# Two early attention batches by head halves and tile pairs, and another order of the first loads

## The chip, the cores and the metric

The kernel runs on one core of one Trainium2 chip. The metric is the device time in microseconds (us) from the start to the end of one execution; lower is better. The core has the engines PE (matrix products), DVE, ACT and POOL (element-wise work), and SP, which here only issues DMA. POOL issues DMA too, in a queue of its own, for transfers that change the type on the way. Every engine works through its own queue in order and waits at semaphores for the others.

## The reference

Linear attention with cosine weights, then a gated feed-forward layer. B, H, S, D are 8, 8, 576, 64; the layer goes from 512 to 2048 and back.

```python
theta = np.pi / 2.0 * np.arange(S) / S
def phi(x, c, s):
    r = np.maximum(x, 0.0)
    return np.concatenate([r * c, r * s], axis=-1)
q_p, k_p = phi(q, cos_w, sin_w), phi(k, cos_w, sin_w)
kv = np.einsum('bhsf,bhsd->bhfd', k_p, v)
z = np.sum(k_p, axis=2)
num = np.einsum('bhsf,bhfd->bhsd', q_p, kv)
den = np.einsum('bhsf,bhf->bhs', q_p, z)[..., None] + 1e-06
x = (num / den).transpose(0, 2, 1, 3).reshape(B * S, H * D)
h = x @ w_in
out = (h * np.cos(h)) @ w_out
```

## The kernel before

Each batch of 576 rows is cut into four tiles of 128 tokens and a rest of 64; the rests of all batches form a ninth batch for the layer alone. For one batch the steps are: SP loads q, k, v in float32 (`load`, L318 and L321, two DMAs each; v of batches 0 and 1 in two halves of four heads). DVE or ACT makes a feature from a tile (`prep`, L346 on ACT, L347 on DVE: relu, times the cosine or sine column, 512 wide for eight heads). v is cast to 16 bits (`cast_v`, L360 to L362). PE transposes q's features (`q_pe`, L402) and ACT or DVE copies them out of PSUM into `qT` (L406, L408). PE sums k's features times v over the tiles (`kv`, L373), and the sum goes to `kvz` (L385, L387, L390). PE multiplies `qT` by `kvz` (`num`, L435); DVE adds 1e-6 to the denominator, takes its reciprocal and multiplies (L451, L453, L455: the norm, into `x16`). PE transposes the result (`x_pe`, L475) and ACT copies it to `xT` (L479). Layer 1 of batches 0 and 1 (`layer1`, L529) makes blocks of eight matmuls of 256 columns; ACT takes the cosine (L502), DVE multiplies (L504) into `gT`. Layer 2 of batch 0 (`layer2_plain`, L786) makes blocks of eight matmuls of 512 columns, four with the first half of `w_out` and four with the second; ACT stores the first half's sum (L794), DVE adds the second (L797). Later batches use Strassen-like products: sums of weights (`w_out_sums`, L809; `w_in_sums`, L603) and L667, L679, L861, L872, L883.

PSUM has eight banks: three `M1`, two `M2`, one `TR`, two `ATT`. `num` of batches 0 and 1 uses `ATT` and, by turns, a pair of the others.

The order is written out. Each step is added to a plan with the engines that may do it; the tables `STARTS` and `ENGS` give each step its place and its engine, and steps are issued in the order of `STARTS`. What a step waits for follows from the data it reads and writes.

Batch 0 loads q, k, v in this order. While they come, PE runs matmuls on constants (`warm`, L945: 28, then 17, then 9 more between the steps of `num`). POOL copies an element of k into `w_in_sb` (L950): this makes the four loads of `w_in` (L956) wait for k. A copy of a loaded element of `w_in` in the same way releases half of `w_out` (L960, L970). An element of `w_in`'s third quarter releases batch 1's loads (`hold_raw`, L975), and an element of batch 1's q the second half of `w_out` (`part_of_w_out`, L982).

## Time and profile before

| | |
|---|---|
| three timed runs, us | 281.47, 281.58, 283.69; median 281.58 |
| profiled execution: its span, us | 279.7 |
| instructions | 6825 |
| PE, DVE, ACT, POOL busy, us | 272.6, 236.9, 210.2, 82.9 |
| warm-up matmuls of L945 | 9.04 us for the first 28, 3.67 us for the next 17 |
| HBM read and written, MB | 36.75 and 11.80 |
| DMA queue of POOL, of SP | 17.04 MB and 39.99 MB |

The profile is of one execution; of its own time the page gives the span alone, which lies 1.9 us under the median of the timed runs. PE's busy time holds the warm-up matmuls, which compute nothing. Line numbers L are those of the kernel before, up to the result. "Idle before, releaser" names what an engine waited for. The time of a DMA is counted from its issue to its landing, so a wait in a queue is in it.

### The profile page before, as it was taken

How to read it: one execution, taken by the hardware profiler on the slowest of the kernel's cores; microseconds unless marked ns; L12 is line 12 of the kernel's file. 1: busy time of each engine (PE TensorE's matmuls, PEld its weight loads, DVE VectorE, ACT ScalarE, POOL GpSimd, SP SyncE). 2: the span in 40 equal slices, each digit the busy share in tenths (PEclk: the TensorE clock that was granted, in tenths of full speed). 3: DMA queues.
4: the chain of work that ended last, by engine and by line, in shares of the span. 5: the costliest groups of instructions: out<-in, count | busy, mean ns of one | idle time of the engine just before them, and what ended most of it. 6: DMA issues, size and time to landing. Idle time of an engine off the chain costs nothing.

```text
span 279.7 us, 6825 instructions
## 1 busy us (share of the span) xinstructions
PE 272.6 (97%) x2698; PEld 215.5 (77%) x2698; DVE 236.9 (85%) x442; ACT 210.2 (75%) x363; POOL 82.9 (30%) x102
## 2 busy tenths in 40 slices
PE   8999999999999999999999999999999999999993
PEld 2567857787966677769777878789988888888882
DVE  1767698989999999999999998989989879873952
ACT  2756699879998897788989988995758686776330
POOL 1430020030501201520340045132534372399210
PEclk9999999999999999999999999999999999999999
DMA  6999989999999999989999998549756495698125
GB/s 207 312 202 206 340 239 241 361 301 174 335 261 271 258 249 246 234 268 259 255 258 246 242 229 284 98 115 141 163 75 139 110 156 105 152 143 123 75 77 150
DMA packets 80223, 58.03 MB, mean 207 GB/s; under 512 B 43200, under 2 KB 77248, under 8 KB 80192
## 3 DMA queue, kind: packets, MB, share of 16 engines
q1 hardware_dynamic: 68960, 39.99, 59.4%
q0 software_dynamic: 10496, 17.04, 30.1%
q10 hardware_dynamic: 736, 0.57, 0.7%
q8 instruction: 21, 0.34, 0.5%
q14 instruction: 10, 0.08, 0.1%
HBM read 36.75 MB, written 11.80 MB: 174 GB/s over the span
## 4 chain that ended last, share of the span: by engine, by line
PE 92%; ACT 3%; DVE 2%; issue 1%; POOL 0%; ACTq 0%; POOLq 0%
PE M L861 34%; PE M L667 14%; PE M L561 11%; PE M L529 9%; PE TR L667 6%; PE ATT L945 5%; PE ATT L435 3%; PE M L786 3%; PE ATT L373 3%; PE TR L561 2%; ACT KQ L346 2%; DVE x L455 1%; PE M L402 1%; PE M L373 0%; PE TR L475 0%
## 5 line engine op out<-in xcount | busy, mean ns | idle before, releaser
L861 PEld LDWEIGHTS <-gT 128*128 128x128 f16 x560 | 53.9, 98 | 8.3
L861 PE MATMUL M<-w_out_sb,gT 128*128 128x256 f16 x448 | 57.1, 273 | 0.0
L504 DVE TENSOR_TENSOR gT<-M,ch 128x512 f16<-128x512 f32 x73 | 48.5, 685 | 5.9 <-ACT ch L502 5.7
L502 ACT ACTIVATE ch<-M 128x512 f32<-128x512 f32 x75 | 43.4, 596 | 12.0 <-PE M L529 5.4
L346 ACT ACTIVATE KQ<-km,CS 128x512 f16<-128x512 f32 x57 | 38.5, 717 | 1.4 <-DMA km<-in_k_dram 1.3
L872 ACT ACTIVATE ost<-M 128x512 f32<-128x512 f32 x41 | 24.3, 596 | 17.9 <-PE M L861 13.0
L346 ACT ACTIVATE KQ<-qm,CS 128x512 f16<-128x512 f32 x46 | 31.5, 720 | 4.1 <-DMA qm<-in_q_dram 4.1
L561 PE MATMUL M<-xT,w_in_sb 128*128 128x512 f16 x136 | 33.8, 379 | 0.0
L861 PE MATMUL M<-T,S 128*128 128x256 f16 x256 | 32.4, 273 | 0.0
L667 PEld LDWEIGHTS <-w_in_sb 128*128 128x128 f16 x288 | 27.3, 98 | 4.8 <-issue 0.3
L362 POOL CAST V<-vm 128x1024 f16<-128x1024 f32 (+1 forms) x18 | 15.9, 907 | 50.8 <-DVE den L451 20.7
L529 PE MATMUL M<-xT,w_in_sb 128*128 128x256 f16 x256 | 30.3, 273 | 0.3 <-DVE gT L504 0.3
L861 PEld LDWEIGHTS <-S 128*128 128x128 f16 x256 | 24.8, 98 | 4.1 <-DVE S L837 0.2
L529 PEld LDWEIGHTS <-w_in_sb 128*128 128x128 f16 x256 | 24.4, 98 | 3.9 <-issue 0.5
L679 DVE TENSOR_TENSOR Z<-M,Z 128x512 f32<-128x512 f32 x31 | 21.1, 687 | 4.3 <-PE M L667 3.1
L561 PEld LDWEIGHTS <-w_in_sb 128*128 128x128 f16 x160 | 14.9, 98 | 12.2
L504 POOL TENSOR_TENSOR gT<-Z,ch 128x512 f16<-128x512 f32 x5 | 6.3, 1268 | 56.6 <-ACT ch L502 20.0
L455 DVE TENSOR_TENSOR x<-ATT,rec 128x512 f16<-128x512 f32 x32 | 22.1, 691 | 1.1
L435 PEld LDWEIGHTS <-qT 128*128 128x128 f16 (+1 forms) x320 | 14.8, 101 | 5.6 <-issue 3.5
L690 ACT ACTIVATE ch<-Z 128x1024 f32<-128x1024 f32 x12 | 12.7, 1057 | 6.9 <-DVE Z L679 4.8
L675 ACT ACTIVATE Z<-M 128x512 f32<-128x512 f32 x26 | 15.1, 596 | 3.4 <-PE M L667 2.4
L435 PE MATMUL ATT<-kvz,qT 128*128 128x65 f16 (+1 forms) x288 | 16.0, 195 | 0.8 <-DVE x L455 0.5
(150 smaller groups left out, 519.3 us busy)
## 6 DMA issues: line engine op xcount, KB each, us to landing
out_dram<-ost POOLq DMA_DIRECT2D x38, 256.0 KB, 4.3
qm<-in_q_dram SPq DMA_DIRECT2D x8, 640.0 KB, 6.7
km<-in_k_dram SPq DMA_DIRECT2D x8, 640.0 KB, 7.1
qm<-in_q_dram SPq DMA_DIRECT2D x8, 512.0 KB, 6.0
km<-in_k_dram SPq DMA_DIRECT2D x8, 512.0 KB, 6.0
vm<-in_v_dram SPq DMA_DIRECT2D x6, 640.0 KB, 5.7
vm<-in_v_dram SPq DMA_DIRECT2D x6, 512.0 KB, 4.6
w_in_sb<-in_moe_w_in_dram POOLq DMA_DIRECT2D x4, 512.0 KB, 8.8
```

The source lines that it names most:

```text
L346: fn = {"ACT": lambda: nc.scalar.activation(out=out_, in_=in_, func=AF.Relu, scale=sc), "DVE": lambda: nc.vector.tensor_scalar(out=out_, i ...
L362: "POOL": lambda: nc.gpsimd.tensor_copy(out=out_, in_=in_)}
L435: nc.tensor.matmul(bank[hb][ps, hh * D1:(hh + 1) * D1], lhsT=x[:, h, :], rhs=z[:, h, :], start=True, stop=True)
L455: nc.vector.tensor_tensor(out=split(x16[n][:, hs, :], k), in0=A[:, :, :, 0:D], in1=split(rec[n][:, hs], k).unsqueeze(3).broadcast_to((P, k ...
L502: act(0.5, due, lambda: nc.scalar.activation(out=ch[c], in_=bank, func=AF.Sin, bias=math.pi / 2.0, scale=1.0), [key], [("ch", c)])
L504: mul(due, 0.61, lambda q: q.tensor_tensor(out=dst, in0=bank if len(dst.shape) == 2 else bank.rearrange("p (j s) -> p j s", j=dst.shape[1] ...
L529: nc.tensor.matmul(M1[m][:, jj * 2 * P:(jj + 1) * 2 * P], lhsT=w_in_sb[:, cc, j * P:(j + 1) * P], rhs=X[:, cc, ts], start=(cc == 0), stop= ...
L561: nc.tensor.matmul(M, lhsT=w_in_sb[:, cc, j * P:(j + 1) * P], rhs=X[:, cc, :], start=(cc == 0), stop=(cc == NCT - 1))
L667: nc.tensor.matmul(bank[0][:, j * TH:(j + 1) * TH], lhsT=a(cc, j), rhs=b[:, cc, :], start=(first and j == 0 and cc == 0), stop=(last and j ...
L679: dve(0.61, due + 0.3, lambda: nc.vector.tensor_tensor(out=dst, in0=bank[0], in1=dst, op=ALU.add), [bank[1], key], [key])
L861: nc.tensor.matmul(bank[0][:, tt * MH:(tt + 1) * MH], lhsT=a[:, j, tt * P:(tt + 1) * P], rhs=b[:, j, :], start=(first and (apart or tt == ...
L872: act(0.5, due, lambda: nc.scalar.activation(out=dst, in_=view(bank), func=AF.Copy), [bank[1]], dk)
```

## The change

The names in the built program stay, its functions are new for batch 0 and partly for batch 1:

- Batch 0: features of k, casts of v, kv, num and x are made for four heads at a time (`half_tiles`, called for each half). kv of a half starts when that half's features and casts are there. `num_pair` computes one half of the heads for two tiles into the two `ATT` banks and normalizes both at once; `x_pair` transposes two tiles of a half into one bank. Several copies may be done by either engine; the table says by which.
- Batch 1: kv by halves, then `num_pair` and `x_pair` by tile pair and half.
- `w_in`'s four loads wait for a feature of q (tile 1, cosine) over two copies on POOL, in place of an element of k.
- All four loads of `w_out` follow `w_in`; batch 1's loads wait for the third group of `w_out`.
- Layer 1 of batches 0 and 1 runs over the halves of the columns before it goes to the second half of the tiles: quarters 0, 1 for the first two tiles, then for the last two, then quarters 2, 3.
- `STARTS` and `ENGS` are new for the whole kernel. The other options of `OPT` are off. `WS2`, which would put a hold in front of the second half of `w_in`, is `None`; the table places those two loads after casts of v, on a queue that has no other step there.

```diff
+OPT = dict(F16=0, WS2=None, HQ=[1, 0, 1], ..., HH='kv', LD=[['q', 3], ['k', 3], ['v', 0], ['v', 1]], NB=...,
+           XB=[['B3'], ['B3', 'M1']], W0=5, W1=6, WF=[[2, 2], [2, 2]], ..., P0=1, RAW1=6, WO2=-1, H1=2, ...)
...
-    GATE1 = (w_in_sb[0:2, 0, Dff // 2 + 1:Dff // 2 + 2], [("w_in", 2)])
+    GATE1 = ((w_in_sb[...], [("w_in", R1)]) if R1 < 4 else
+             (w_out_sb[0:2, (R1 - 4) * NJT // 4, 1:2], [("w_out", R1 - 4)]))
...
-            for quarter in range(4):
-                for hf in range(2):
+            for quarter, hf in ([(q_ + i, hf) for q_ in (0, 2) for hf in range(2) for i in range(2)] if OPT["HH"] else
...
     def weights():
...
+            t, g, hops = OPT["HQ"]
+            src, rd = qp[0:2, t, 0, g, 0:1], [("qp", t, g, 0)]
+            for i in range(hops):
+                pl.add("POOL", 0.4, 0.5, 0, lambda i=i, src=src: nc.gpsimd.tensor_copy(out=HP[:, i:i + 1], in_=src),
+                       rd, [("hop", i)])
+                src, rd = HP[:, i:i + 1], [("hop", i)]
+            pl.add("POOL", 0.4, 0.5, 0, lambda src=src: nc.gpsimd.tensor_copy(
+                out=w_in_sb[0:2, 0, :].rearrange("p (g f) -> p g f", g=4)[:, :, 0],
+                in_=src.broadcast_to((2, 4))), rd, [("w_in", g_) for g_ in range(4)])
...
+        w_in_load(range(2 if OPT["WS2"] else 4))
+        if not OPT["WS2"]:
+            weights2()
...
-            w_out_load(0, 2)
+            w_out_load(0, 2 if HOLDW >= 0 else 4)
...
+    def kv_half(hb, bank, key, due, b=0):
...
+            for hh, h in enumerate(hs):
+                for t in range(NT + 1):
+                    nc.tensor.matmul(
+                        bank[:, hh * D1:(hh + 1) * D1], lhsT=kp[:, t, h].rearrange("p g d -> p (g d)"),
+                        rhs=V1[:, t, h, :], start=(t == 0), stop=(t == NT))
...
+        copy_by_either(Z[:, hb], bank[:, 0:HB * D1], due, 0.4, 0.38, [key], [("kvz", b, hb)])
...
+    def num_pair(i, hb, due, b=0):
+        hs = HALVES[hb]
+        for t in (2 * i, 2 * i + 1):
+            bank, key = ATT[:, t % 2, :], ("ATT", t % 2)
...
+                for hh in range(HB):
+                    nc.tensor.matmul(bank[:, hh * D1:(hh + 1) * D1], lhsT=qT[t][:, hb * HB + hh, :],
+                                     rhs=kvz[b][:, hb * HB + hh, :], start=True, stop=True)
...
+        def norm():
+            nc.vector.tensor_scalar_add(out=denp[:, n], in0=A[:, :, :, D], scalar1=1e-6)
+            nc.vector.reciprocal(out=recp[:, n], in_=denp[:, n])
+            nc.vector.tensor_tensor(out=XF[:, hb, 2 * i:2 * i + 2], in0=A[:, :, :, 0:D],
+                                    in1=recp[:, n].unsqueeze(3).broadcast_to((P, 2, HB, D)), op=ALU.mult)
...
+    def x_pair(i, hb, bank, key, due, b=0):
...
+            for j in range(2):
+                x2 = XF[:, hb, 2 * i + j].rearrange("p h d -> p (h d)")
+                for c in range(NCT // 2):
+                    nc.tensor.matmul(ps[:, c, j * P:(j + 1) * P], lhsT=x2[:, c * P:(c + 1) * P], rhs=IDENT,
+                                     is_transpose=True)
...
+    def half_tiles(hb, due):
...
+        for nm in OPT["HH"]:
+            if nm == "k":
+                for t in range(NT + 1):
+                    for g in range(2):
+                        prep(0, "k", t, g, "", due, hs)
+            elif nm == "v":
+                for t, nt in ((0, 2), (2, 2), (4, 1)):
+                    cast_v(0, t, ("DVE", "ACT", "POOL"), due, hs, nt=nt)
+                kv_half(hb, *BANKS2[hb], due)
...
+            for i in range(NT // 2):
+                num_pair(i, hb, due + 2 * i)
+                n = OPT["WF"][hb][i]
+                if n:
+                    warm(n, 0.2157 * n, M1[1], [("ATT", 1)], [("M1", 1)])
+                x_pair(i, hb, *pick[kb_[i % len(kb_)]], due + 2 * i)
...
     def second_attention():
...
+            for hb in range(2):
+                kv_half(hb, ATT[:, hb, :], ("ATT", hb), T + 6, 1)
+            if OPT["H1"] == 2:
+                for i in range(NT // 2):
+                    for hb in range(2):
+                        num_pair(i, hb, T + 8 + 2 * i, 1)
+                        x_pair(i, hb, *(BANKS[3], BANKS[2])[hb], T + 8 + 2 * i, 1)
```

More of the change, by code (lines that the diff above doesn't have):

```diff
@@ L344, in prep @@
         f = len(heads) / H
[L345 removed]
+        cost = {"DVE": 0.09 + FD * f, "ACT": 0.12 + 0.5 * f}
         fn = {"ACT": lambda: nc.scalar.activation(out=out_, in_=in_, func=AF.Relu, scale=sc),
@@ L398, in q_pe @@
         ps = bank.bitcast(F16).rearrange("p (h s) -> p h s", h=H)
+        more = [("qTh", t % NT, hb) for hb in range(2)] if b <= 1 and OPT["HH"] else []
         def mm():
@@ L577 @@
     LATE = min(c for c, nf in FAST1.items() if nf > 2)
-    assert all(FAST1[c] == NJT // 4 for c in range(LATE, NC))
     def flat(t, dt=F16):
```

376 lines of the change are left out of this document (309 added, 67 removed), and 196 rows, old and new, of the table STARTS.

## The prediction

> **What bounds the kernel now.** I read first the busy times by stage, to see which part of the span can still give time. Columns: the stage in us, its length, then busy us (and instructions) of PE, weight load, DVE, ACT, POOL, then granted clock, DMA share, GB/s.
>
> ```profile
> 0.00:24.00 24.00, 21.84 (x192) 12.63 (x193) 14.00 (x40) 12.40 (x22) 6.26 (x14) 1.00 1.02 236
> 24.00:34.00 10.00, 10.00 (x93) 8.82 (x92) 6.92 (x10) 6.73 (x13) 0.54 (x4) 1.00 1.16 285
> 34.00:60.00 26.00, 25.75 (x273) 17.93 (x271) 24.51 (x59) 22.78 (x41) 4.45 (x6) 1.00 1.00 281
> 60.00:80.00 20.00, 20.00 (x259) 16.86 (x256) 18.18 (x34) 19.11 (x35) 4.76 (x7) 1.00 1.10 291
> 80.00:275.00 195.00, 194.98 (x1890) 159.30 (x1888) 172.82 (x300) 149.15 (x256) 66.92 (x71) 1.00 0.86 183
> ```
>
> From 60 us on PE has no hole (194.98 of 195 us). Its matmuls there are the same in both programs, so the end moves by what PE gains or loses before 60 us, one for one. Two stretches can change: up to 24 us, where PE mostly runs warm-up matmuls (L945) while batch 0 arrives, and 34 to 60, where DVE and ACT are nearly full with batch 1. The chain that ended last shows both:
>
> ```profile
> 11.25 3.67 PE ATT L945 x17
> ...
> 23.88 10.72 PE M L529 x96
> 34.67 0.45 issue
> 35.12 1.60 ACT KQ L346 x3
> ...
> 43.70 0.57 ACT kvz L390
> 44.31 0.29 PE ATT L435 x4
> ```
>
> Layer 1 is dense from 23.88; from 35 to 44 the chain runs through ACT, batch 1's features. Then the timeline of the start, for arrivals and durations:
>
> ```profile
> 7.25 2.07 DVE L347 TENSOR_SCALAR KQ<-qm,CS 128x512 f16<-128x512 f32 x5 [5.27 <-DMA qm<-in_q_dram]
> ...
> 10.53 2.21 DVE L347 TENSOR_SCALAR KQ<-km,CS 128x512 f16<-128x512 f32 x5 [1.21 <-DMA km<-in_k_dram]
> 10.57 0.19 POOL L950 CAST w_in_sb<-km 2x4 f16<-2x4 f32 x1 [9.09 <-DMA km<-in_k_dram]
> ...
> 11.13 3.46 POOL L956 DMA_DIRECT2D w_in_sb<-in_moe_w_in_dram  x4 [0.37 <-POOL w_in_sb L950]
> ```
>
> q is usable at 7.25, k at 10.53, and w_in is issued at 11.13, released by k. Last, DMA by the microsecond:
>
> ```profile
> 27.00:28.00 1.00, 1.00 (x12) 0.89 (x10) 0.82 (x2) 0.72 (x2) 0.00 (x0) 1.00 1.26 209
> 28.00:29.00 1.00, 1.00 (x12) 0.90 (x10) 0.78 (x2) 0.72 (x2) 0.00 (x0) 1.00 1.23 207
> 29.00:30.00 1.00, 1.00 (x12) 0.90 (x10) 0.69 (x1) 0.71 (x2) 0.00 (x0) 1.00 1.12 319
> 30.00:31.00 1.00, 1.00 (x12) 0.90 (x10) 0.80 (x2) 0.60 (x1) 0.00 (x0) 1.00 1.09 382
> ```
>
> Weights move at 205 to 209 GB/s, raw q, k, v at 355 to 388. Batch 1's k is issued at 25.88, yet the weight rate stays until 29: raw data queued behind weights waits until these have run out.
>
> **Part 1, batch 0 by head halves.** q's features and transposes stay; SP's eight loads keep their order, so q, k, v arrive as before. After k, only half of the heads stands ahead of the first kv product. Of shapes not in the trace: a 128x256 feature on DVE lies between half of 0.414 (2.07/5) and the 0.28 to 0.29 of the 128x256 cast; I take 0.25, in the middle, as the cast has fixed cost too. On ACT I take 0.41, from that engine's 128x256 casts (0.402 to 0.425). By the new order on the queues, DVE does seven half features from 10.53 (to 12.28), then casts of 0.28 and 0.42: 12.98. ACT, held by two qT copies of 1.02 until 10.66, does four features and a cast of 0.65: 12.95. kv of half 0: 20 x 0.031, to 13.75 with its drain. ACT has three features of half 1 queued ahead of the kvz copy: it ends at 14.6. num on PE, then a norm, which in the trace takes 1.11 (den at 18.84 to the end of x at 19.95, the same 512 columns): 15.1 to 16.2. Half 1's ten features and casts fill the gaps; kv of half 1 runs at 16.5, its kvz ends at 17.65. The second norm waits for ATT and ends at 17.8; DVE copies xT (0.42, between half of and the full 0.69 of the 128x1024 copy), third norm 18.3 to 19.4, x transposes, xT copy to 20.3. Layer 1 starts at 20.4; its first four blocks need only tiles 0, 1, and the fourth norm (to 21.4) hides beside them: blocks at 20.4, 21.27, x transposes of 0.23, 22.38, 23.25, fifth at 24.12. Before, blocks start at 21.20, 22.36, 23.88, 24.75, fifth at 25.63. Gain **1.5 us**. With the ends of the bounds (0.21 or 0.29 per half feature over some 11 in a row on DVE, xT copies of 0.35 or 0.69) it is 1.0 to 2.1. The 14 warm-up matmuls left out (40 for 54) cost and bring nothing: none stands ahead of waiting work.
>
> **Part 2, w_in and w_out.** The q feature that releases w_in is DVE's fifth: 9.32. Two POOL copies of 0.19, each followed by the 0.3 to 0.37 seen after L950, put the first issue at 10.5: **0.6 us** earlier. Four issues take 3.46 as now. In the built program all four stand one behind the other on POOL with no wait between: the half "behind the v casts" is not held by anything. The full weight rate came 3 us after issue (11.13, 184 GB/s from 14), so now from 13.6, after batch 0's last raw packets (333 GB/s until 13): v keeps its time.
>
> All four w_out groups now follow w_in, and batch 1's loads are released by the sixth of the eight groups instead of the fourth of six. Groups land 2.7 us apart (w_in's first at 11.13 + 6.1 = 17.2, w_out's second at 18.5 + 12.3 = 30.8: 13.6/5). Raw data still waits until the weight queue is empty, which is two groups later, 5.15 by rate (2 x 524 KB / 0.205), less 0.6: batch 1 comes **4.55 us later**. Before, by the issues' landing times, q is there at 27.92 + 9.9 = 37.8, v's halves at 39.4 and 32.95 + 8.0 = 40.95; now 42.4, 44.0, 45.5. SP issues them behind the same waits as before. The hole in DMA at 39 to 41 (74 and 46 GB/s), before the second half of w_out, closes; batch 2 gains, which nobody waits for (PE full from 60).
> New dates for w_out: its group 1 lands seventh, at 30.8 - 0.6 + 2.7 = 32.9; PE's first layer-2 block comes at 24.12 + 11 x 0.873 = 33.7. Cover 0.8; beyond it each us counts. DVE's first w_out sum needs the last group, 35.6, and stands at about 36; a miss is covered, since k's features can't start before 38.5.
>
> **Part 3, batch 1.** Six layer-2 blocks (1.73 each) now stand ahead of its transposes, where two stood (three ahead of its kv): PE arrives at 24.12 + 12 x 0.873 + 6 x 1.73 = 45.0. DVE is the pace: q's six features from 42.5 at 0.45 (0.42 to 0.53 in the rows) to 45.2, four V casts to 46.6, qT copy 0.69, kvz copy 0.43, a layer-2 sum 0.69 queued ahead of the first norm, norm 48.5 to 49.65. PE runs two transposes, kv at 46.0 and 46.7, num at 47.9, a transpose, and from 48.6 stands until 49.7, because num of half 1 needs ATT back. Then two layer-2 blocks cover the other norms; layer 1 of batch 1 starts at 54.6. PE's work from the fifth block to there is 12 x 0.873 + 8 x 1.73 + 4 x 0.45 + 40 x 0.031 + 8 x 0.125 + 3 x 0.23 = 29.05 of 30.5: 1.4 lost. Before, the same count is 24.07 of 50.27 - 25.63 = 24.64: 0.57 lost. Cost **0.85 us**; by earlier or later arrival 0 to 2.5.
> From 60 us on, the new table only permutes the same work under a full PE: nothing, bounds 0.5 either way.
>
> **Sum.** -1.5 + 0.85 = -0.65 on the profiled span of 279.7: 279.05. The span lies 1.9 under the median of 281.58, and I keep that distance: **280.9**. Less than 1% (2.8 us) can hardly be told from no change here.
>
> **Rivals.**
> A, the start's gain stays: batch 1 arrives before PE needs it, loses no more than 0.57, and the start gives its 2.1: 279.5; with batch 1's stall gone too, 278.9. For it: DMA has no hole now. Against: DVE, 24.51 of 26 us busy in that stage already, gets the same features later.
> B, slower: batch 1's raw data. It waits for the slowest DMA engine's last weight packet, and groups land 2.7 apart where the rate alone gives 2.56; with eight queued at once this can spread further. The point is q at 42.5, since DVE's row runs without slack from there; each us later costs one. Half a group to two groups late, 1.6 to 5.4 us: 282.5 to 286.3. Against: the queue keeps 196 to 211 GB/s in every us from 15 to 29.
> C, the change doesn't do what it says: the second half of w_in isn't held and takes engines from batch 0's v. If the two took turns from 12.4 on (10.5 and the 1.9 from L956's issue to the end of the raw rate), v's second half would come up to 0.5 later, 0.4 of it past the casts before it: 281.3. If w_in took them whole, v would come after its 10 us: 291. Against both: v is queued first, and from 25.88 to 29 order of arrival decided.
> The Trainium skill, page "DMA: Bandwidth & Descriptors", section "Queues, rings and completion order", states the turns: each engine goes round its queues packet by packet. The 207 GB/s at 28 to 29, with raw loads issued since 25.88, disagree.
> D, the clock. Warm-up matmuls run at 0.427 apart until 7.2, later 0.216. Now 16 stand at the start, to 7.7, then pieces with holes up to 1.1 us. Were the clock to fall back, each us of such work doubles; over some 3 us, 282.4. The granted clock in the stages above is 1.00 throughout.
> The Trainium skill, "TensorE: Matmul & The Clock Gate", section "Part 1: The HAM clock gate", wants a whole idle window of about 3.4 us for that, an estimate by which D stays out; no run here shows it yet.
>
> **How the numbers follow.** Forecast 0.42 (own range 280.1 to 281.7), A 0.23, B 0.21, C 0.09 (turns 0.06), D 0.05. Half of A, where the new table helps too, passes 1% (278.8); two fifths of B and C's worse half lie over 284.4: faster 0.12, same 0.76, slower 0.12. The range 278.6 to 284.6 leaves out a third of A, two fifths of B, and 291: not quite 0.2.
>
> **What would show it.** Layer 1's first block near 20.4, and dense from there; w_in issued near 10.5; raw rate for batch 1 from 34; first q feature of batch 1 near 42.5; PE waiting on a norm near 49; layer 1 of batch 1 near 54.6. I am wrong if v's second half in batch 0 lands after 14, if PE waits for w_out before 34, or if PE has holes after 60.

## The result and the profile after

The changed kernel takes 283.35 us (median of 5 runs, 283.04 to 283.57), the kernel before 282.08 in the same comparison (281.47 to 283.69). The ratio is 1.0045, with a 95% interval of 1.0026 to 1.0064: slower by 0.45%, where 0.65 us of gain had been forecast. The profiled execution took 283.3 us with a span of 281.4, so 1.9 us lie around the span, as before.

The busy times by stage, of the kernel after (columns as before: stage, length, then busy us of PE, weight load, DVE, ACT, POOL, then clock, DMA share, GB/s):

```profile
0.00:24.00 24.00, 20.26 (x184) 11.82 (x185) 15.66 (x41) 12.62 (x24) 7.83 (x17) 1.00 1.03 245
...
34.00:60.00 26.00, 24.66 (x254) 16.14 (x252) 22.17 (x52) 20.13 (x34) 1.87 (x3) 1.00 0.85 282
60.00:80.00 20.00, 18.82 (x257) 16.91 (x255) 17.79 (x35) 18.70 (x35) 5.42 (x8) 1.00 1.11 280
80.00:275.00 195.00, 194.99 (x1897) 159.12 (x1894) 172.45 (x299) 151.98 (x261) 66.77 (x71) 1.00 0.87 185
```

From 80 us on PE is full, as it was. Between 60 and 80 it now has a hole of 1.2 us that the kernel before did not have (20.00 of 20), and from 34 to 60 it works 1.1 us less. The chain that ended last, of the kernel after, names the places:

```profile
10.46 1.61 DVE KQ L363 x5
...
45.90 0.89 PE M L422 x16
46.79 1.22 PE ATT L1171 x40
51.29 1.73 PE M L871 x8
53.49 1.73 PE M L871 x8
...
67.26 1.17 ACT KQ L362 x2
68.73 6.92 DMA qT<-KQ
```

At the start the chain runs through DVE's k features, no longer through ACT's features of batch 1 at 35 to 44. Layer 1 is dense again from about 23.3. Then there is a piece that is new: a DMA transpose of batch 2's q, 6.92 us long, ends at 75.65 on the chain. PE's timeline of the kernel after shows what each costs; the brackets hold the idle time ahead of the row and what ended it:

```profile
48.94 0.41 PE L1223 MATMUL ATT<-kvz,qT 128*128 128x65 f16 x8 [0.49 <-ACT kvz L1150]
...
50.65 0.29 PE L1223 MATMUL ATT<-kvz,qT 128*128 128x65 f16 x4 [0.85 <-DVE XN L1232]
...
75.69 0.43 PE L458 MATMUL ATT<-kvz,qT 128*128 128x65 f16 x8 [1.13 <-DMA qT<-KQ]
```

The timeline of the start, kernel after (start, us, engine and line, operation, and in brackets the idle time ahead):

```profile
7.18 2.46 DVE L363 TENSOR_SCALAR KQ<-qm,CS 128x512 f16<-128x512 f32 x6 [5.20 <-DMA qm<-in_q_dram]
...
10.25 3.16 POOL L1061 DMA_DIRECT2D w_in_sb<-in_moe_w_in_dram  x4 [0.31 <-POOL w_in_sb L1049]
...
10.46 2.58 DVE L363 TENSOR_SCALAR KQ<-km,CS 128x256 f16<-128x256 f32 x7
```

The seven half-width features take 0.369 us each, where I had taken 0.25. They stand exactly beside POOL's four issues of w_in. And DMA by the microsecond, kernel after: the weights' rate holds until 33, then raw data moves.

```profile
32.00:33.00 1.00, 1.00 (x12) 0.90 (x10) 0.82 (x2) 0.64 (x2) 0.00 (x0) 1.00 1.25 208
33.00:34.00 1.00, 1.00 (x12) 0.89 (x10) 1.00 (x3) 0.72 (x2) 0.00 (x0) 1.00 1.08 277
34.00:35.00 1.00, 1.00 (x10) 0.70 (x8) 1.00 (x3) 0.72 (x2) 0.00 (x0) 1.00 1.09 347
```

The account against the kernel before, by the two profiles:

| stretch | before | after | change |
|---|---|---|---|
| fifth layer-1 block of batch 0 starts | 25.63 | 24.90 | -0.73 (forecast -1.5) |
| from there to layer 1 of batch 1, less PE's work | 0.57 lost | 30.63 - 29.05 = 1.58 lost | +1.0 (forecast +0.85) |
| PE's hole at 75.69 | none | 1.13 | +1.1 (forecast 0) |
| 55.5 to 60.4, DVE's features ahead of an xT copy and gates | | | some +0.3, taken as the rest of the 1.7 between the spans |

### The profile page after: what moved, and what is told of

Same layout as the page of the kernel before. It is cut to its first block, busy times and chain, and to the rows that moved or that the text cites. A ratio compares the mean times of both kernels' runs of the same rounds, so it can differ in the third digit from the quotient of the medians.

```text
span 281.4 us, 6809 instructions
## 1 busy us (share of the span) xinstructions
PE 270.4 (96%) x2684; PEld 214.2 (76%) x2684; DVE 237.5 (84%) x437; ACT 211.0 (75%) x363; POOL 82.4 (29%) x102
## 4 chain that ended last, share of the span: by engine, by line
PE 86%; DMA 5%; DVE 5%; ACT 1%; issue 1%; SPq 1%; DVEq 0%
PE M L946 34%; PE M L730 14%; PE M L602 11%; PE M L569 7%; PE TR L730 6%; PE M L871 5%; DMA km<-in_k_dram 3%; PE ATT L391 3%; PE ATT L458 3%; DMA qT<-KQ 2%; PE TR L602 2%; DVE KQ L363 1%; PE ATT L1223 1%; DVE XN L1232 1%; PE M L1171 1%
## 5 line engine op out<-in xcount | busy, mean ns | idle before, releaser
L362 ACT ACTIVATE KQ<-km,CS 128x512 f16<-128x512 f32 (+1 forms) x63 | 40.9, 686 | 0.0
L362 ACT ACTIVATE KQ<-qm,CS 128x512 f16<-128x512 f32 x45 | 30.6, 721 | 4.0 <-DMA qm<-in_q_dram 4.0
L602 PE MATMUL M<-xT,w_in_sb 128*128 128x512 f16 x136 | 33.4, 379 | 0.0
L602 PEld LDWEIGHTS <-w_in_sb 128*128 128x128 f16 x160 | 15.0, 98 | 12.6
L815 POOL DMA_DIRECT2D out_dram<-ost x20 | 11.1, 554 | 31.2 <-DVE ost L882 24.4
L479 DVE TENSOR_TENSOR XN<-ATT,rec 128x512 f16<-128x512 f32 x28 | 19.4, 691 | 1.0
L363 DVE TENSOR_SCALAR KQ<-qm,CS 128x512 f16<-128x512 f32 x27 | 11.9, 480 | 5.7 <-DMA qm<-in_q_dram 5.5
```

Of the source, the lines that this page charges most:

```text
L362: fn = {"ACT": lambda: nc.scalar.activation(out=out_, in_=in_, func=AF.Relu, scale=sc), "DVE": lambda: nc.vector.tensor_scalar(out=out_, i ...
L479: nc.vector.tensor_tensor(out=split(x16[n][:, hs, :], k), in0=A[:, :, :, 0:D], in1=split(rec[n][:, hs], k).unsqueeze(3).broadcast_to((P, k ...
L602: nc.tensor.matmul(M, lhsT=w_in_sb[:, cc, j * P:(j + 1) * P], rhs=X[:, cc, :], start=(cc == 0), stop=(cc == NCT - 1))
```

## The experiments

In one profile q arrives at 7.14, in another at 8.03; all that follows moves with it. So I read distances, not dates: from DVE's first q feature to the first layer-1 block (the start), from the third layer-1 block of batch 0 to the first of batch 1 (batch 1), and from there to the first layer-1 block of the later form, L602 of the kernel after (the stretch to 80 us). PE's work in each distance is the same in all rows, save where a note says otherwise.

| run | start | batch 1 | to 80 us | time | ratio to before (95%) |
|---|---|---|---|---|---|
| the changed kernel | 14.00 | 32.38 | 24.71 | 283.35 | 1.0026 to 1.0064 |
| w_in late | 13.09 | weights late | | 284.51 | one run |
| w_in by raw q | 13.38 | 32.39 | 23.41 | 282.60 | 0.9995 to 1.0030 |
| whole features | 13.62 | 32.39 | 23.77 | 282.84 | 1.0005 to 1.0040 |
| both of these | 13.64 | 32.39 | 24.02 | 282.81 | 0.9997 to 1.0037 |
| both, norms in another order | 12.03 | more work inside | 23.42 | 282.48 | 0.9990 to 1.0022 |
| raw data early | 13.99 | 32.39 | 24.00 | 283.44 | 1.0026 to 1.0053 |
| short norms | 13.99 | 31.94 | 24.06 | 283.06 | one run |
| batch 1 in another order | 13.99 | 30.45, less work inside | 26.65 | 284.07 | 1.0060 to 1.0103 |
| fourth transpose first | 13.99 | 32.38 | 25.16 | 286.30 | 1.0129 to 1.0171 |
| this and batch 1's order | 14.05 | 30.45 | 28.09 | 285.75 | 1.0105 to 1.0141 |
| v load ahead | 14.04 | 32.38 | 24.09 | 283.62 | 1.0029 to 1.0071 |
| v load ahead, norm first | 14.07 | 32.39 | 24.51 | 284.53 | 1.0063 to 1.0087 |
| this and w_in by raw q | 13.38 | 32.38 | 24.38 | 283.33 | 1.0009 to 1.0046 |
| q features first | 13.99 | 32.38 | 24.43 | 283.34 | 1.0036 to 1.0087 |
| the kernel before, w_in by raw q | 13.48 (13.95 without) | | | 281.60 | 0.9962 to 0.9995 |

The table ends at 80 us, and PE is not full behind it in every run. From the first of the later blocks (L602) to the last block of PE it is 194.52 us in the changed kernel, and about as much in most runs; it is 195.49 with w_in by raw q, 195.77 with both edits, 195.54 with the v load ahead and the norm first, and 196.20 with the fourth transpose first. In these four PE waits for later transposes between 92 and 111 us.

### The start: what made the half features slow

Two theories for the 0.369 us: the shape has that much fixed cost, or POOL's issue of w_in beside it slows DVE. In the first run POOL's release waits for a V cast (and the weights' steps follow batch 0's first half), so that POOL is silent while DVE makes the features.

```diff
...
-            src, rd = qp[0:2, t, 0, g, 0:1], [("qp", t, g, 0)]
+            src, rd = V1[0:2, 2, 0, 0:1], [("V1", 2, 0)]
...
```

> w_in's issue is released by the V cast of batch 0's first head half (about 13.9 us) and not by a q feature (9.3), so that POOL issues nothing while DVE makes the half-width k features between 10.4 and 13. Everything else has the changed kernel's order. Theory 'fixed cost' (a 128x256 feature costs 0.34 us on DVE because of its fixed part): the seven features take 7 x 0.34 = 2.38 us, DVE's V casts end at 13.65, first kv at 13.7; the start gains 0.2 us from it, no more. Theory 'issue' (POOL's descriptor writing for w_in, which the change moved onto these features, slows them from 0.25 to 0.37): they take 1.75 us, casts end at 13.0, first kv at 13.1. The time itself is worse in both, since the weights come about 4.3 us later: w_in's second quarter lands near 23.5 and w_out's groups near 31 to 39, so that layer 1 and the first layer-2 blocks wait: 2 to 5 us longer, 285 to 288.

The timeline of this run:

```profile
10.75 1.93 DVE L368 TENSOR_SCALAR KQ<-km,CS 128x256 f16<-128x256 f32 x7
...
14.02 3.21 POOL L1066 DMA_DIRECT2D w_in_sb<-in_moe_w_in_dram  x4 [0.31 <-POOL w_in_sb L1054]
```

Seven features in 1.93 us, 0.276 each: the theory of the issue is right, and that of the fixed cost falls. The start shrinks from 14.00 to 13.09. The time is longer, as expected, since the weights are late (PE waits 1.17 us for w_out). The Trainium skill, page "SBUF — State Buffer", section "SBUF: two separate sides", says that DVE and GpSimd share one pair of ports under an exclusive lock, which a DVE instruction asks for in a 2-port mode or with two inputs in SBUF; the later one is blocked. The trace agrees in sign: 0.276 against 0.369, single features up to 0.62. That it is this lock was not shown.

The next run goes the other way: raw q itself releases w_in, so that POOL's issues stand mostly ahead of the k features, not beside them. POOL's steps move up in the table to follow it.

```diff
...
-            src, rd = qp[0:2, t, 0, g, 0:1], [("qp", t, g, 0)]
+            src, rd = raw["q"][0:2, 0, 0, 0:1], hk("q", [0], [0])
```

> w_in's issue is released by raw q itself (7.2 us) and not by the fourth of DVE's q features; nothing else is changed. The four issues on POOL then stand at 8.0 to 11.2 beside the q features and not at 10.25 to 13.4 beside the k features. Theory 'issue' (POOL's issue slows DVE's features): q's six take up to 0.5 us longer (2.46 now), the seven k features 2.0 to 2.2 in place of 2.58, casts end near 13.5, first kv at 13.5; the start gains 0.3 to 0.5. On DMA: if packets go by order of arrival, v still lands by 13.5 since all its loads are issued before; the weights and with them w_out and batch 1's raw data come up to 2.2 us earlier. If weights and raw data took turns, v's second half would land 0.5 to 2 us later and the first kv with it, past 14. Time: 282.3 to 283 if v is undisturbed (start 0.4, batch 1 up to 0.5), 283.5 to 285 if v is late.

Its timeline:

```profile
7.28 2.59 DVE L374 TENSOR_SCALAR KQ<-qm,CS 128x512 f16<-128x512 f32 x6 [5.30 <-DMA qm<-in_q_dram]
...
8.13 3.52 POOL L1072 DMA_DIRECT2D w_in_sb<-in_moe_w_in_dram  x4 [0.31 <-POOL w_in_sb L1060]
...
10.55 2.26 DVE L374 TENSOR_SCALAR KQ<-km,CS 128x256 f16<-128x256 f32 x7
```

The issue now lies mostly on q's features (2.59 us for 2.46) and only its end on k's (2.26 for 2.58). The start gains 0.62. The medians differ by 0.75; by the ratios to the kernel before, 1.0045 and 1.0012, it is 0.9. In its profile the stretch to 80 us is 1.30 shorter as well, and 1.0 is lost again behind 80, 0.48 of it in a wait for a transpose at 92.58. v's casts did not wait (v's last load landed 8.2 us after its issue, 8.0 in the changed kernel), and w_in's first quarter still lands near 16.1 (the copy behind it runs at 16.13, 16.09 in the changed kernel): weights issued two microseconds sooner did not move sooner, as raw data filled the engines until 13. The start's gain is DVE's alone: 0.32 in the k features, 0.27 in the two V casts behind them (0.62 for 0.89).

One by one, DVE's instructions tell how the issue acts. Of the timeline, the changed kernel's long ones, then one of the run with w_in by raw q:

```profile
10.73 0.52 DVE L363 TENSOR_SCALAR KQ<-km,CS 128x256 f16<-128x256 f32 x1
11.42 0.62 DVE L363 TENSOR_SCALAR KQ<-km,CS 128x256 f16<-128x256 f32 x1
12.22 0.56 DVE L363 TENSOR_SCALAR KQ<-km,CS 128x256 f16<-128x256 f32 x1
12.96 0.57 DVE L377 CAST V<-vm 128x256 f16<-128x256 f32 x1
...
11.68 0.33 DVE L374 TENSOR_SCALAR KQ<-km,CS 128x256 f16<-128x256 f32 x1
```

The other four features of the changed kernel take 0.33 to 0.35, as all seven do with POOL silent, and that cast takes 0.29 there. (Taken one by one, each time overlaps the next by some 0.07 us, so they add up to more than the 2.58 of the row above.) So it is not each instruction that slows: four issues of w_in go with four long instructions, 0.2 to 0.3 us too long each. A rival is that the weights' packets slow DVE, not their issue. It falls: w_in's first packets move only after 12 in both runs, and the changed kernel's first two long features come before that. With w_in by raw q the issue ends at 11.65, and the four features that start behind it take 0.33 to 0.34 each, packets or not.

Whole features avoid half of the instructions: DVE makes five of the ten k features 128x512, once for all heads, and takes two V casts over from ACT.

```diff
...
+                        whole = (t, g) in WHOLE
+                        if not whole or hb == 0:
+                            prep(0, "k", t, g, "", due, slice(0, H) if whole else hs)
-                        prep(0, "k", t, g, "", due, hs)
```

> Only batch 0 is changed: five of the ten k features (those of tiles 0, 1, 2 and 4 that DVE makes) are made for all heads at once, 128x512, ahead of the first kv; ACT makes the other five by head halves; two V casts of the second half go from ACT to DVE, which has four features less later. In the run with w_in released late the seven half-width features took 1.93 us (0.276 each) where the changed kernel takes 2.58 (0.369 each), so that POOL's issue of w_in is what slows them. Theory 'per instruction' (what POOL's issue costs DVE goes by instructions or by pauses between them): five whole features take 2.1 to 2.3 us as the five of the kernel before did beside the same issue (2.21), casts end near 13.5, first kv at 13.6 in place of 13.91, and with DVE's later work gone the first layer-1 block comes 0.5 to 0.8 earlier (20.4 to 20.7): 282.6 to 282.9. Theory 'per time' (DVE loses a share of the time, whatever the shapes): five whole features take 2.07 x 2.58/1.93 = 2.8 us, first kv at 14.1, the start gains 0 to 0.3. Should the chain through the norms (1.13 each, one after the other) bind rather than the features, less than 0.3 is gained in any case.

The row of these features in this run's timeline:

```profile
10.66 2.32 DVE L377 TENSOR_SCALAR KQ<-km,CS 128x512 f16<-128x512 f32 x5
```

They take 0.464 us each, where q's whole features take 0.41. That is at the upper end of the expected 2.1 to 2.3, but the start gains 0.38, not 0.5 to 0.8; that the chain of norms holds the rest is argued here. Both edits together, with the expectation for them:

> The edits of the two runs that helped together: w_in released by raw q, and five of batch 0's k features made whole on DVE with two V casts taken over from ACT. Counted from q's arrival, the first layer-1 block came at 14.00 us in the changed kernel, at 13.38 with w_in released by raw q and at 13.62 with whole features. Theory 'issue' (both runs remove the same loss, DVE's features beside POOL's issue): the gains do not add, the block comes at 13.3 to 13.4, the time is that of the run with w_in released by raw q, 282.6 within 0.3. Theory 'two losses' (whole features also take DVE's and ACT's later work off the second half): the block comes at 13.0, 282.2.

13.64 is worse than w_in by raw q alone (13.38). The gains don't add: both remove the same loss. Then the norms of batch 0 in another order on top, both head halves of tiles 0 and 1 first (`pair(1)` of both halves is emitted behind `pair(0)` of both):

> As the run with both edits, and the four norms of batch 0 in another order: both head halves of tiles 0 and 1 first, so that layer 1 starts after the second norm and not after the third; the norms of tiles 2 and 3 stand beside the first four layer-1 blocks (two pieces of warm-up are left out). If the chain through ATT (num, norm of 1.13 us, num again) sets the start once the features are out of the way, the second head half's kvz near 17.0 gives norms at 15.3, 17.5, an xT copy to 19.6 and the first block 12.3 to 12.6 us after q's arrival, 1 us earlier than with the old order of norms: 281.3 to 281.8, below the kernel before. If the fifth block then waits for the last norm, 0.3 to 0.7 of it is given back: 281.7 to 282.3. If PE's holes at 60 to 100 us (transposes, loads) take it, nothing: 282.4 to 282.8.

The start is 12.03, better than expected, and the time is no better than with w_in by raw q (282.48 and 282.60, intervals that overlap). PE's timeline of this run tells why:

```profile
19.29 1.24 PE L615 MATMUL M<-xT,w_in_sb 128*128 128x256 f16 x8
20.75 0.40 PE L1291 MATMUL TR<-IDENT,XN 128*128 128x128 f16 x4 [0.22 <-DVE XN L1278]
...
34.00 1.89 PE L917 MATMUL M<-w_out_sb,gT 128*128 128x512 f16 x8
```

Layer 1 starts 1.4 us sooner, but the first layer-2 block stands at 34.00, as with w_in by raw q (33.98, q 0.02 later there). PE's nums and x transposes of tiles 2 and 3, done before in time in which PE stood anyway, now lie between the layer-1 blocks. What counts is not when the first block starts but when PE is full for good. Of the outcomes expected, the time is the last one's (282.4 to 282.8), for another reason than holes behind 60 us.

Last of this group, the same early release in the kernel before, again with POOL's steps moved up:

```diff
...
-                in_=raw[ORDER0[1]][0:2, 0, 0, 0:1].broadcast_to((2, 4)))
+                in_=raw[ORDER0[0]][0:2, 0, 0, 0:1].broadcast_to((2, 4)))
```

> The kernel before, with one edit: w_in's issue is released by raw q (7.3 us) and not by raw k (10.5), so that POOL's four issues stand at about 7.8 to 11.3 and not at 11.13 to 14.59. Theory 'issue' (POOL's issue slows whatever DVE does beside it): here the five k features (2.21 us for 2.07 without it) and the V casts are freed, 0.2 to 0.3 us, and w_in's first quarter lands up to 1 us earlier; since the norms of this kernel follow each other in full, 0.2 to 0.4 us of it reach layer 1: 281.9 to 282.2 beside 282.4. If the release is worth its 0.6 us only beside half-width features, nothing: 282.4 within 0.2. Slower only if the weights take engines from batch 0's v: then v's second half lands past 13.5 and the start loses 0.3 or more.

281.60 against 282.42, ratio 0.9978 (0.9962 to 0.9995): this is the fastest kernel of the study, faster than both. The issue cost the kernel before as well; the change did not bring this loss, it moved it to where DVE had more and shorter instructions in a row. Its five k features themselves took as long as before (2.20 us); the three V casts behind them took 0.69 for 0.88 and the feature after that 0.48 for 0.61. The price that the expectation had named, v late, was paid too. From the timeline of this run:

```profile
14.97 0.70 DVE L365 CAST V<-vm 128x256 f16<-128x256 f32 x3 [0.86 <-DMA vm<-in_v_dram]
```

v's last load landed 8.8 us after its issue, 8.0 in the kernel before, where no cast waited. Even so the start is 0.47 shorter; by which step is not shown.

### Batch 1: late data or an exposed chain

The forecast had two reasons for the loss at batch 1: DVE gets the data late and is full, and PE's waits on kvz and on the first norm have no cover left. The first test brings the raw data sooner: its loads are released by w_in's fourth group.

```diff
-... RAW1=6, ...
+... RAW1=3, ...
```

> Batch 1's raw loads are released by w_in's fourth group and not by w_out's sixth in line, some 5 us earlier (25 in place of 30.27); nothing else is changed. By order of arrival nothing moves sooner: the raw packets still start near 33.3 behind w_out's last group, the time is the changed kernel's 283.35 within 0.3. If the queues took turns, raw packets would move from 26 at a share of the engines, q's features of batch 1 could start up to 4 us earlier, and w_out's groups would land 2 to 5 us later, with PE waiting at its first layer-2 block (34.5): then 'late data' would lose less at batch 1 (layer 1 of batch 1 less than 30.0 us after the fifth block, 30.63 now) and more ahead of it, 283 to 287.

DMA by the microsecond in this run:

```profile
29.00:30.00 1.00, 1.00 (x12) 0.90 (x10) 0.82 (x2) 0.68 (x2) 0.00 (x0) 1.00 1.18 208
30.00:31.00 1.00, 1.00 (x11) 0.90 (x10) 0.82 (x2) 0.72 (x2) 0.00 (x0) 1.00 1.20 256
31.00:32.00 1.00, 1.00 (x11) 0.90 (x10) 0.82 (x2) 0.72 (x2) 0.00 (x0) 1.00 1.12 236
```

I was wrong about the order of arrival. Loads issued at 25.45 move from 29.4, while weights are still queued: from 30 to 36, raw data (120 to 140 KB per us) and weights (about 120) share the engines about equally, though all of these weights were issued by 19.9. The Trainium skill, page "DMA: Bandwidth & Descriptors", section "Queues, rings and completion order", says that the engines take turns, packet by packet, and this run agrees; the prediction had set it aside. In the kernel before and after, the weights happened to run out 3 to 4 us after the raw loads were issued, which looks the same. What the 4 us from issue to first packet are stays open.

The sharing made w_out late (DVE's first sum of w_out waited 2.63 us), and with it q's features. DVE's rows of this run and of the changed kernel:

```profile
44.00 2.46 DVE L365 TENSOR_SCALAR KQ<-qm,CS 128x512 f16<-128x512 f32 x6
...
41.72 2.47 DVE L363 TENSOR_SCALAR KQ<-qm,CS 128x512 f16<-128x512 f32 x6 [0.33 <-DMA qm<-in_q_dram]
```

They start 1.8 us later once batch 0's arrival of q is taken off. And the distance of batch 1 is 32.39, to 0.01 us what it was. So features 1.8 us later cost nothing; late data is not the cause, and DVE's row had slack.

The second test shortens the norm alone, which leaves out a part of the computation.

```diff
+            if b == 0:
-            nc.vector.tensor_scalar_add(out=denp[:, n], in0=A[:, :, :, D], scalar1=1e-6)
-            nc.vector.reciprocal(out=recp[:, n], in_=denp[:, n])
+                nc.vector.tensor_scalar_add(out=denp[:, n], in0=A[:, :, :, D], scalar1=1e-6)
+                nc.vector.reciprocal(out=recp[:, n], in_=denp[:, n])
```

> The changed kernel, but batch 1's four norms leave out the addition and the reciprocal of the denominators and multiply by batch 0's: a part of the computation is left out, and each norm is about 0.45 us shorter on DVE; the order is the same on all engines. Theory 'exposed chain': PE's wait on the first norm falls from 0.85 to 0.4, and layer 1 of batch 1 comes 0.45 to 0.9 us sooner after the fifth block (32.38 us after the second block in the changed kernel, 31.5 to 31.9 here). Rival 'DVE full': the later features only move up, and PE's waits stay within 0.1 of 1.34.

```profile
49.78 0.41 PE L1225 MATMUL ATT<-kvz,qT 128*128 128x65 f16 x8 [0.49 <-ACT kvz L1152]
...
51.04 0.29 PE L1225 MATMUL ATT<-kvz,qT 128*128 128x65 f16 x4 [0.40 <-DVE XN L1235]
```

PE's wait falls from 0.85 to 0.40 and the distance from 32.38 to 31.94: what the norm loses, batch 1 gains, one for one. The exposed chain it is; the wait of 0.49 on kvz, another part of it, was not tested by itself. Can another order cover it? Here a transpose of q and a layer-2 block fill the two waits (and layer 1 starts ahead of the last norms):

```diff
+for _n, _s in {186: 4660, 243: 4718, 236: 4730, 241: 4883, 209: 5090, 247: 5110, 253: 5112, 248: 5290, 249: 5299}.items():
+    STARTS[_n] = _s
...
```

> Batch 1's attention in another order, the start and SP's order as in the changed kernel. On PE one more transpose of q goes ahead of the first num, the first of the two remaining layer-2 blocks stands right behind that num (it stood behind the second), the second one before the third num, and layer 1 of batch 1 starts before the last norms; one output sum moves behind the first norm on DVE, one copy of qT goes to ACT. Theory 'exposed chain' (the 1.58 us that PE loses between the fifth block at 24.90 and layer 1 of batch 1 at 55.53 are PE's waits of 0.49 on kvz and 0.85 on the first norm with its cover queued behind them): layer 1 of batch 1 starts at 54.4 to 54.7. Rival 'late data' (DVE and ACT get batch 1's features 4 us later and are full, so that any order loses the same): it starts at 55.2 to 55.6. The time: if the transposes at 60 to 69 us follow the work before them, 1.0 us less than the changed kernel (282.4); if the hole at 75.69 is set by a transpose that does not move, the gain is lost in that hole, which grows from 1.13 to about 2.1 us, and the time stays within 0.3 us of 283.35.

Layer 1 of batch 1 starts 1.9 us sooner, and PE then stands four times. PE's timeline of this run:

```profile
54.69 1.69 PE L585 MATMUL M<-xT,w_in_sb 128*128 128x256 f16 x14 [0.30 <-DVE xT L1165]
...
57.54 0.61 PE L438 MATMUL TR<-IDENT,KQ 128*128 128x128 f16 x8 [0.69 <-ACT xT L1166]
58.44 0.40 PE L1261 MATMUL M<-IDENT,XN 128*128 128x128 f16 x4 [0.29 <-DVE XN L1248]
59.56 1.03 PE L585 MATMUL M<-xT,w_in_sb 128*128 128x256 f16 x8 [0.72 <-DVE xT L1165]
```

2.0 us of holes in place of 1.34, and 0.7 us more time than the changed kernel. In the two profiles batch 1 and the stretch to 80 us together take the same (57.10 and 57.09), as the hole at 75 is gone here; where the 0.7 between the medians lies is not shown by them. Two layer-2 blocks are left as cover for four norms; in both orders tried, some norm stands bare. In the kernel before, PE had only two of the eight layer-2 blocks ahead of batch 1's transposes, in the changed one six. So w_out ahead of batch 1 costs by letting PE use up its cover, and not by late data; the first half of this is read from the order, the second is shown.

### 60 to 80 us: a row on SP, or full engines

In the changed kernel SP issues three transposes of batch 2's q (from 60.74), two loads of batch 3's v, then the fourth transpose (68.73), for which PE waits. The kernel before has one v load ahead of the transposes (58.28), the fourth transpose at 66.83 with 4.9 us to landing. SP's rows of the fourth transpose, before and after:

```profile
66.83 1.29 SPq L412 DMA_TRANSPOSE qT<-KQ  x1
...
68.73 2.72 SPq L435 DMA_TRANSPOSE qT<-KQ  x1
```

First test: the fourth transpose ahead of the loads, `STARTS[332]` from 6592 to 6310.

> One place in SP's order is changed: batch 2's fourth transpose of q goes ahead of both loads of batch 3's v; all else is as in the changed kernel. Theory 'queue' (the hole of 1.13 us that PE has at 75.69 us in the changed kernel comes from the second v load, which the new table put ahead of that transpose: issued 68.73, 6.92 us to landing): the transpose is issued near 66.6 us, right behind the third one, lands by 73.5, the hole at 75.69 is gone, and the time falls by 1.1 us (0.8 to 1.2) to about 282.2, level with the kernel before. Rival 'stores' (the two output stores that now move at 64 to 68 us slow the transposes): the transpose still takes its 7 us from a start that is little earlier, the hole shrinks by no more than 0.4 us, the time by 0 to 0.4. Rival 'late features': the transpose waits for ACT's q features, so that it is still issued after 68: no change.

None of the three theories holds. The hole at 75 goes, but SP spends 8.75 us on the four transposes and issues v at 69.98 and not at 66.58. PE's timeline of this run, with what it then waits for:

```profile
78.34 0.22 PE L397 MATMUL ATT<-V,KQ 128*128 128x65 f16 x2 [0.77 <-POOL V L384]
78.89 0.64 PE L397 MATMUL ATT<-V,KQ 128*128 128x65 f16 x16 [0.34 <-POOL V L384]
```

It goes on behind 80 us, with waits for transposes of 0.27 at 95.56 and 0.55 at 110.64; 286.30. With batch 1's other order on top:

> The edits of the two runs before together. If 'queue' and 'exposed chain' both hold, PE gains 1.1 at 75.69 and 1.0 before 55.53: 2.1 us less than the changed kernel, 281.2, some 0.9 below the kernel before. If only one holds, 282.2 to 282.4. If neither, 283.3. If the transposes still bind when PE comes 1 us earlier, a hole of 0.3 to 1 us stays near 75: 281.5 to 282.2.

285.75, between its two parts (284.07 and 286.30): neither of the two gains is there. PE again waits ahead of batch 3's kv, 0.77 at 79.34, which the profile puts down to ACT, and 0.34 on V. Next, v's side as in the kernel before: POOL's V casts ahead of two q features on DVE, and one v load ahead of the transposes.

```diff
...
+for _n, _s in {317: 5522, 316: 5523, 315: 5524, 324: 5790, 328: 5791, 435: 5820}.items():
+    STARTS[_n] = _s
```

> Batch 2's V casts on POOL (58.67 to 61.27 in the changed kernel, with their data there since 56.2) stand behind a DVE feature of q by the kernel's own rule for the port that both share; here they are ordered ahead of two q features, which move behind three gate products, and the first of batch 3's two v loads goes ahead of batch 2's three q transposes on SP, as in the kernel before. Theory 'SP's chain' (the hole of 1.13 us at 75.69 is there because casts 3 us later than before (55.65 there) push that v load behind the transposes, so that four transposes and two v loads stand in a row of which the last is needed): casts start at 57.4, the v load is issued near 60, the fourth transpose near 67.3 and not 68.73, and PE has no hole over 0.3 us between 60 and 80: 1.1 us less than the changed kernel, 282.2. Rival 'lateness alone' (every engine is 2 to 3 us behind the table since batch 1, and something else is then last): another hole takes its place near 77 to 79, on V as in the run with the transpose first, and the time stays within 0.4 us of 283.35.

The casts start at 58.00 and the load is issued at 60.63, the transpose only at 69.26; there is no hole at 75, but one of 0.52 at 63.27, on a norm that I had put behind the features. 283.62: nothing gained. With that norm back in front (324 and 328 at 5850 and 5851), and then with w_in by raw q as well:

> As the run with the first v load ahead of the transposes, but without its side effect on DVE: the norm of batch 1's fifth tile stays ahead of the two q features, which now stand right behind it (in that run it came behind them, and PE stood 0.52 us for it at 63.27). Theory 'v load ahead' (in the changed kernel both v loads of batch 3, 1.15 MB, run ahead of the fourth transpose, in the kernel before one, 0.51 MB; the other 0.64 MB at 355 to 390 GB/s are 1.7 us of its 6.9 us to landing, 4.9 in the kernel before): the fourth transpose lands 5 to 5.6 us after its issue, before PE needs it; no hole over 0.2 us at 60 to 80; from layer 1 of batch 1 to the first block of the next layer 1 (24.71 us in the changed kernel's profile, 24.0 in that of the run with raw data early) 23.3 to 23.6; the time 282.6 to 283.0, 0.4 to 0.8 below the changed kernel. Rival 'lateness alone': another wait takes the place, 24 us or more, 283.2 to 283.6.

> The changed kernel with w_in released by raw q and with the v load ahead of the transposes, both as in their own runs. If the two losses are separate places, the start's 0.6 us and what the transposes cost (0.4 to 0.8) add up: 282.0 to 282.4, level with the kernel before or 0.3 below. If the second only shows when the first is there (with w_in released by raw q alone no hole was left at 75), it is the time of that run, 282.6 within 0.2.

284.53 and 283.33. Now the first num waits, 0.56 us at 67.78, as the three transposes take SP 7.07 us behind the v load, 5.73 without it. In the first of the two, 24.51 us to 80 is no longer than in the changed kernel; 1.0 of its 1.2 us more is lost behind 80, 0.36 of it in a wait for a transpose at 94.56. The theory of the v load falls. Its last form was that the row simply starts too late, since ACT's q features are late:

```diff
...
+for _n, _s in {322: 5573, 327: 5574}.items():
+    STARTS[_n] = _s
```

> The changed kernel with one edit on ACT: two more of batch 2's q features (of tiles 0 and 2) go right behind the first one, ahead of the gates of two layer-1 blocks. In the changed kernel the first transpose of q waits for such a feature until 60.74 and the first num that reads it stands at 66.20, 5.46 us later; in the kernel before it is 59.80 and 67.42, 7.62. Theory 'row starts late' (no order of the four transposes and two v loads on SP helps, since the row starts too late for its length): the first transpose is issued 0.8 to 1.3 us sooner, near 59.5 to 59.9, the fourth near 67.5 to 68, the hole at 75.69 is gone, time 282.6 to 283.0. Rival 'ACT full': the gates behind the features come 1.3 us later and PE waits for its banks at 57 to 60 for as long as is gained at 75: 283.2 to 283.8, with the hole moved there.

The row starts at 59.82 (60.74), the fourth transpose at 68.16 (68.73), the hole at 75 is gone, and the time is 283.34. PE's timeline of this run:

```profile
61.67 1.91 PE L576 MATMUL M<-xT,w_in_sb 128*128 128x256 f16 x16 [1.08 <-DVE gT L550]
```

1.08 us, for a gate whose ACT part stands behind the three features. The rival "ACT full" had said just that. So this much is shown: every other order tried has waits of 0.4 to 1.3 us between 55 and 80 us, on transposes, on V, on a norm or on a gate; what is put first is paid for by what comes behind it. ACT and DVE have little time left there (in the kernel after ACT is busy 18.70 and DVE 17.79 of 20 us at 60 to 80, and 0.95 to 1.00 of each us from 56 to 61). But being full is no cause by itself: in the kernel before they were busier at 60 to 80, 19.11 and 18.18, and PE had no hole. That the leftover of batch 1, 1.0 us later against the table than in the kernel before, is what fills them is argued, not shown. How large the loss is stays open too: the order of the changed kernel itself gave 24.71, 24.00 and 23.77 us in three profiles (its own, raw data early, whole features), and 23.41 with w_in by raw q, where the fourth transpose needed 5.9 us to landing, not 6.9. It is a close race, won or lost by what DMA does in that execution.

## Why the prediction was wrong

**The start: the mechanism was right, one term was mis-sized.** "A 128x256 feature on DVE ... I take 0.25" (bounds 0.21 to 0.29) measured 0.276 with POOL silent, inside the bounds, and 0.369 beside POOL's issue of w_in. With POOL silent the start is 13.09 us from q, and the prediction's own chain, 20.4 - 7.25 = 13.15, is right to 0.1. The step that failed stands in part 2: w_in "0.6 us earlier" was priced on POOL and DMA only. The rows of the kernel before already had the sign of it, features at 0.442 beside the issue and 0.414 without; I passed over the difference. Seven features 0.12 slower are 0.83; the gain came out 0.73 and not 1.5, below the lower bound of 1.0.

**w_in and v: right.** Issue at 10.25 (10.5 forecast), v undisturbed, no half of w_in held back. Rival C did not occur in the change, and hardly with w_in issued at 8.13 (v's last load 0.2 later); in the kernel before with w_in issued at 8.19 that load came 0.8 later and casts waited 0.86, more than the 0.5 that C gave for turns. So the reason given, order of arrival, is wrong: where weights run first, the queues share.

**w_out and raw data: dates right, price wrong.** Raw rate from 34 (33.3 to 34), q usable at 42.5 (41.72), no wait for w_out at the first layer-2 block (34.50). Rival B's "each us later costs one" from q at 42.5 on is wrong: features 1.8 us later cost nothing. (Half a group of 2.7 us is also 1.35, not the 1.6 with which its range begins.)

**Batch 1: the size right, the pace not.** +0.85 forecast, +1.0 measured, with PE's wait where it was put (standing from 48.6 to 49.7, in the profile 49.8 to 50.65, and 0.49 ahead of it). The short-norm run shows the norm's part one for one. But "DVE is the pace" is wrong. DVE's row of the first norm, kernel after:

```profile
49.46 0.17 DVE L1230 TENSOR_SCALAR den<-ATT 128x8 f32<-128x8 f32 x1 [0.40 <-PE ATT L1223]
```

DVE waits for PE here, and before that 0.82 and 0.96 us ahead of its qT and kvz copies. The norm's date hung on PE's arrival (45.74, forecast 45.0), not on q's features, so the close number is in part luck.

**"From 60 us on ... nothing, bounds 0.5": failed.** This is the second step that failed, by 0.4 to 1.1 us. A full PE in the kernel before was taken as proof that PE sets the pace there, whatever the table. It was full by a narrow margin: from the issue of the first transpose to the num that reads it the kernel before had 67.42 - 59.80 = 7.62 us, the changed kernel has 66.20 - 60.74 = 5.46. The fourth, for which PE then waited, had 73.65 - 66.83 = 6.82 for a landing of 4.9; in the changed kernel PE was ready 5.83 after its issue (75.69 - 1.13 - 68.73), and it took 6.92. I had not looked at how late each wait was met. Why it took 6.92 and not 4.9 stays open. The clock (rival D) stayed at 1.00.

**Sum.** -0.73 + 1.0 + 1.1 and some 0.3 around 56 to 60 make the 1.7 us between the two spans; between the medians it is 1.27. The 283.35 lies inside the range given, in its upper half, on the other side of no change than the forecast.

## What to carry to other kernels

Price a DMA issue from GpSimd on the vector engine too: look at which instructions run beside it, and move the issue to where the vector engine has slack; here an earlier release, one line and its place in the table, was worth 0.75 to 0.9 us to the changed kernel and 0.6 to 0.8 us to the old one, by ratios and by medians. Starting a stage sooner gains only what the engine that sets the end is idle in; work that filled its waits will lie in its dense part afterwards. Before calling a stretch bound by one engine, measure how closely the other waits in it are met: here a transpose that had landed 1.9 us before its use became a wait of up to 1.1 us, once what stands ahead of it came later.

## What the hardware showed unexpectedly

Half-width features on DVE: 0.276 us with POOL silent, 0.369 beside POOL's DMA issues; 128x512 ones 0.41 and 0.464. The mean hides that in the changed kernel each of the four issues went with one long DVE instruction, 0.52 to 0.62 us, and left the others at the 0.33 to 0.35 that all seven take one by one with POOL silent (neighbours overlap by some 0.07). Two DMA queues that both had work moved 120 to 140 and about 120 KB per us side by side, 236 to 259 GB/s together, less than raw data alone (347 to 388). The time from a raw load's issue to its first packet was 3 to 4 us while weights were running. A DMA transpose of q occupied SP for 1.3 to 3.2 us at 60 to 72 us; the fourth took 2.72 in the changed kernel and 1.43 with w_in by raw q, in the same order on SP.
